# A third relu tile, 48 + 1 rows and a second store queue in a planned attention and long-convolution kernel

## The chip, the cores and the metric

The kernel runs on one core of one Trainium2 chip. The metric is the device time of one execution in microseconds (us). The median of three runs before the change is 1019.45 us (1018.49 to 1021.79).

## The reference

Eight batches of 3136 rows and 256 channels. Everything below is done for each batch.

```python
scores = (1 / S) * z @ z.T                     # z: 3136 x 64
out    = u * (np.maximum(scores, 0) ** 2 @ v)  # u, v: 3136 x 256
proj   = out @ w_proj                          # 256 -> 3 * 256
x1, x2, x3 = split(proj)
conv   = irfft(rfft(x2, axis=rows) * rfft(filter_fft, axis=rows))
y      = (x1 * conv * x3) @ w_out
```

## The kernel before

**Attention.** The 3136 rows of a batch are cut into seven chunks of columns (`CHUNKS`: five of 512, one of 256, one of 320), and the keys into 25 tiles of 128 rows, the last of 64. For a chunk, TensorE makes the scores of two key tiles at a time into a pair of PSUM banks (`ps_s`, three pairs). K is only 64 there, so the two tiles lie in the two halves of the array's rows: these matmuls use 64 rows of the array, and most others 128. ScalarE applies relu from PSUM into an f32 tile in SBUF, `R_p` (`relu`, L1759). The square goes from `R` to a bf16 tile `A_p` on VectorE (L1768) or on ScalarE (L1766), as the planner finds better; `relu` is for ScalarE alone. TensorE then weighs v with the squares into two accumulators, `ps_o` (one bank for each half of the 256 channels; `weigh`). Since scores are symmetric, a square of A is also turned by a DMA transpose on SP's queue (`mirror`, L1692) into `M1`, `M2e` or `M2o` and used by a later chunk. At the end of a chunk VectorE multiplies the accumulators with u, transposed by DMA, into `xT` (L1810); that frees the accumulators for the next chunk.

**Projection and convolution.** `add_proj` multiplies `xT` with `w_proj`: two of the three parts are multiplied into a gate tile (`g_p`, L1155), and the third goes through the first stage of a Fourier transform of length 49 x 64 (`dft1`) and is stored to a DRAM scratch, `spec`. When a batch's seven chunks are stored, `add_spectrum` loads that scratch in another order (`load_spec`, rows of one residue together: two times 49 partitions), does the second stage in eight groups of four quadrant matmuls ("quads", 49 or 64 rows, both banks of a pair), multiplies with the filter's transform on VectorE (L1240), does the inverse stage and stores (`put`). `add_end` loads the result by chunk (`load_c`), does the last stage, gates it (L1328), multiplies with `w_out` and stores to the output. PSUM is emptied by ScalarE (L551) or VectorE (L555), whichever the planner takes. The last batch has its own form: the eight groups are loaded one by one into whatever tiles are free, the inverse does the last addition on TensorE, and the chunks end in the order `FINAL`. Four chunks of the batch before it (`HOLD` and up) are held back and fill gaps there.

**The planner.** All of this is entered as tasks with a cost per engine, dependencies and tiles taken and freed (`Plan`). `Plan.go` then plays the engines forward and emits each instruction in the order that results; every engine gets a fixed list. `pick_pe` chooses TensorE's next task among queues: S (scores of a pair), Q (quads), W (weighing), FA, FB and FZ (projection, ends, fillers). It tries not to change between tasks of 64 rows (S, Q) and of 128 rows too often. `pick` chooses for the other engines. `Pairs` and `Singles` are the PSUM banks as the planner sees them; `MOST` is how many single banks may be held at once by tasks that take one. `PACE`, `BACKLOG`, `AMPLE`, `STAY`, `FULL`, `FIRST`, `LEAD` and `YIELD` are weights in these choices. SP's queue carries loads, stores and transposes in its planned order; POOL's carries the loads that convert from f32 to bf16 (v, u, z).

Of the kernel before, what the change touches and what calls it, by code (L numbers as in the profile page):

```python
# [11 lines left out]
P = 128  # L12
# [22 lines left out]
ZP, ZL = 0, 0.0  # L35
MOST = 4
FULL = 3.5
QUAD, FIRST, LEAD = -INF, 0.0, 1
YIELD = 1.0
REACH = 2  # L40
SHARE = {0: 1, 2: 3}

# [140 lines left out]
class Plan:  # L183
# [85 lines left out]
    def queued(self, t):  # L269
        some = {id(x): x for e in ("ACT", "DVE") for x in self.pend[e] if x.ready <= t + 0.3}  # L270
        return sum(max(0.0, self.free[e] - t) for e in ("ACT", "DVE")) + sum(min(x.cost.values()) for x in some.values())

    def pick_pe(self):
        t = self.free["PE"]
        got = {}
# [12 lines left out]
        if self.mode == "S" and self.quarters and quad and quad[0] <= t + STAY:  # L288
            if not more or self.quad_run < 1 and self.score_run >= LEAD:
                return (*quad, "Q")  # L290
        if more and not more[0].left:
            left = self.backlog()
            if self.mode == "S":
                if "S" in got and got["S"][0] <= t + STAY:
                    return (*got["S"], "S")
                got.pop("S", None)
                if self.quarters and quad and quad[0] <= t + STAY and self.quad_run < 1:
                    return (*quad, "Q")
            else:
                want = 3 if left > AMPLE else 2  # L300
                free = self.pairs.when(min(want, len(more)) - 1)
                first = quad and quad[0] <= t + 0.3 and left > FIRST and self.credit > QUAD
                if "S" in got and free > t + 0.04:
                    rest = {k: v for k, v in got.items() if k != "S" and (k == "W" or left > BACKLOG)}
                    if rest and min(v[0] for v in rest.values()) < free:
                        got = rest
                    elif free < INF:
                        if first and not LEAD:
                            return max(quad[0], free), quad[1], "Q"
                        self.soon = bool(first)  # L310
                        return max(got["S"][0], free), got["S"][1], "S"
                elif "S" in got:
                    if first and not LEAD:
# [10 lines left out]
        order += ["FA", "FB", "W", "FZ"] if self.credit > 0 and self.queued(t) < FULL else ["W", "FA", "FB", "FZ"]  # L324
# [28 lines left out]
    def go(self):  # L353
        while True:
# [11 lines left out]
            if k:  # L366
                self.queues[k].remove(task)
                half = k in ("S", "Q")
                if half != (self.mode == "S") and self.mode:
                    start += 0.095 if half or not self.quarters else 0.12  # L370
                    self.quarters, self.quad_run, self.score_run = half and self.soon, 0, 0
# [7 lines left out]
                if k == "W":  # L379
                    self.credit = min(self.credit + PACE, 2.0)  # L380
                elif k != "S":
# [7 lines left out]
def kernel(  # L389
# [587 lines left out]

    def by_row(d, r):
        return d[0:S, :].rearrange("(q r x) d -> r q x d", r=2, x=2 * NJ)[r]

    def load_spec(src, j0, nj, deps, late=0.0, home=l_p):
        box = {}

        def go():
            box["t"] = home.tile([P, 8, D] if home is l_p else [P, 4, D], BF16)
# [5 lines left out]
        t = on("SP", go, 0.9, [*deps, *((d, ISSUED) for d in loads[-1:])], [home.slots], moves=0.6 * nj, late=late)  # L991
        return in_order(t), box
# [216 lines left out]
    def add_spectrum(b, puts):  # L1209
        deps0 = list(h_done) + list(tz_done) if b == 0 else []  # L1210
        final = b == B - 1
        per = 2 if final else 4
        homes = [l_p, c_p, un_p] * 2 + M_p[:2]
        lasts = []
        behind = []
        ldb, gb = [None], [None]
        for g in range(NJ // 2):
            own = not final or g % 2 == 0
            xh, gh = (xh_p, (gs_p, uT_p)[final and g > 3]) if own else (R_p, A_p)
            if 2 * g % per == 0:  # L1220
                ldb[0] = load_spec(D1[b % 2], 2 * g, per, puts, LATE_LOAD * (not final), homes[g] if final else l_p)
            ld, ibox = ldb[0]
            ends_load = (2 * g + 2) % per == 0
            xb = {}

            def mm(ps, g=g, xb=xb, ibox=ibox, xh=xh):
                xb["x"] = xh.tile([P, 2, 4, D], BF16)
                forward(ps, slot(ibox["t"], 2 * g % per), g)

# [3 lines left out]
            a0, evs = add_quads(mm, ev, c_quads(g), [ld, *deps0], [xh.slots])  # L1233
            if ends_load:
                a0.frees.append((ld, 0))
# [15 lines left out]

            def inv(g=g, xb=xb, z_=z_, a0=a0, gh=gh):
                if 2 * g % per == 0:
                    gb[0] = {"es": [], "firsts": []}
                gx = gb[0]
                new = 2 * g % per == 0

# [9 lines left out]
                def ev(e, h, p, g=g):  # L1267
                    copy(e, gx["g"][:, ds(2 * (2 * g % per + h), 2), :].rearrange("p c d -> p (c d)"), p)

# [8 lines left out]
                gx["es"] += evs  # L1278
                if (2 * g + 2) % per:
                    return  # L1280
                j0 = 2 * g + 2 - per

                def put():
                    for r in range(2):
                        nc.sync.dma_start(
                            out=by_row(D2[b % 2], r)[:, ds(2 * j0, 2 * per), :], in_=gx["g"][ds(r * N1, N2), 0 : 2 * per, :]
                        )

                p_ = on("SP", put, 0.8, gx["es"], moves=0.5 * per, late=LATE_D2 * (not final))
                p_.frees.append((gx["g0"], 1))  # L1290
# [9 lines left out]
    def add_end(b, lasts, gtasks, cs, kind="FB", src=c_p, dsts=(o_p,), late=0, behind=(), then=(), split=False, mids=(y_p,)):  # L1300
        for at, c in enumerate(cs):
# [81 lines left out]

            def store(i0, n, c=c, ob=ob):
                r = rows_n1(out[b])
                for j, lo, hi, n2 in runs(T0[c] + i0, T0[c] + i0 + n):
                    nc.sync.dma_start(
                        out=r[:, n2 : n2 + hi - lo, :], in_=ob["o"][ds(j * N1, N1), i0 : i0 + hi - lo, :]
                    )
# [514 lines left out]
```

## Time and profile before

| | before |
|---|---|
| median of three runs | 1019.45 us |
| the profiled execution | 1014.12 us, span 1012.0 us |
| granted TensorE clock, mean | 0.988 |
| TensorE busy | 969.6 us (96%) |
| VectorE busy | 851.8 us (84%) |
| ScalarE busy | 854.2 us (84%) |
| relu from PSUM, 128 x 1024 (L1759) | 408 instructions, 1031 ns each |
| square on VectorE, 128 x 1024 (L1768) | 276 instructions, 1218 ns each |
| square on ScalarE, 128 x 1024 (L1766) | 116 instructions, 1072 ns each |
| DMA moved | 170.29 MB, mean 168 GB/s |

The time of the profiled execution includes about 2 us outside the span from the first to the last instruction. A duration in the table is one instruction from its start to its end; the next one on the same engine can start a little before that end. An engine's waits are put down to what released it.

### The profile page before, as it was taken

The numbers are of one execution on the slowest core, as the hardware profiler recorded it, in microseconds if no ns is written. First come the engines' busy times: TensorE is split into PE (matmuls) and PEld (weight loads), VectorE is DVE, ScalarE is ACT, GpSimd is POOL, SyncE is SP. The second block draws the span as 40 slices with busy tenths as digits, with TensorE's granted clock in tenths as the row PEclk, the third lists the DMA queues.
The fourth block names the chain that finished last, engine by engine and source line by source line (L and its number), as shares of the span: only waits on it lengthen the run. The fifth ranks groups of instructions, "written<-read, shape, count | busy, mean of one in ns | idle before, by whom it ended". The sixth has DMA issues, their size and how long they took to land.

```text
span 1012.0 us, 19360 instructions
## 1 busy us (share of the span) xinstructions
PE 969.6 (96%) x6776; PEld 472.2 (47%) x6776; DVE 851.8 (84%) x1470; ACT 854.2 (84%) x1182; POOL 187.5 (19%) x403
## 2 busy tenths in 40 slices
PE   6999999999999999999999999999999999999985
PEld 2343534446444653346544364434643455444744
DVE  7986699988899778988899688997789988998674
ACT  5886789897999789987889878997889978999673
POOL 5142311132011220313021131111301312000000
PEclk9999999999999999999999999999999999999978
DMA  9699788998999988987879999988899988977556
GB/s 168 130 165 166 121 156 165 165 137 187 185 194 174 196 163 168 172 170 140 203 171 138 170 163 188 196 152 172 186 176 173 162 148 195 173 166 130 158 182 207
DMA packets 331777, 170.29 MB, mean 168 GB/s; under 512 B 241160, under 2 KB 306504, under 8 KB 331680
## 3 DMA queue, kind: packets, MB, share of 16 engines
q1 hardware_dynamic: 303952, 138.09, 65.5%
q0 software_dynamic: 27728, 30.97, 21.6%
q8 instruction: 53, 0.87, 0.4%
q14 instruction: 44, 0.36, 0.1%
HBM read 90.26 MB, written 53.35 MB: 142 GB/s over the span
## 4 chain that ended last, share of the span: by engine, by line
PE 72%; DVE 11%; DMA 7%; ACT 5%; issue 3%; SPq 1%; ACTq 0%; DVEq 0%
PE ps_o_t L518 41%; PE ps_s L518 31%; DVE A_t L1768 5%; ACT R_t L1759 3%; DVE xT_t L1810 2%; DMA zT_t<-zd_t 2%; DMA M2e_t<-A_t 1%; ACT A_t L1766 1%; DVE xh L1240 1%; DMA spec_in_t<-spec 1%; DMA M_t<-A_t 1%; DMA conv_in_t<-spec 1%; DMA ost_t<-in_z_dram 1%; ACT gs_t L551 1%; DMA un_t<-spec 0%
## 5 line engine op out<-in xcount | busy, mean ns | idle before, releaser
L1759 ACT ACTIVATE R_t<-ps_s 128x1024 f32<-128x1024 f32 (+4 forms) x512 | 476.8, 960 | 79.9 <-PE ps_s L518 37.6
L518 PE MATMUL ps_o_t<-A_t,v_t 128*128 128x512 bf16 (+3 forms) x2068 | 463.5, 355 | 5.6 <-DVE A_t L1768 4.5
L1768 DVE TENSOR_TENSOR A_t<-R_t 128x1024 bf16<-128x1024 f32 (+3 forms) x337 | 379.9, 1145 | 56.0 <-ACT R_t L1759 45.7
L518 PEld LDWEIGHTS <-v_t 128*128 128x128 bf16 (+2 forms) x2872 | 247.6, 98 | 280.4 <-issue 87.4
L518 PE MATMUL ps_s<-zT_t 64*64 64x512 bf16 (+4 forms) x1436 | 174.5, 370 | 1.4 <-ACT R_t L1759 0.6
L1766 ACT ACTIVATE A_t<-R_t 128x1024 bf16<-128x1024 f32 (+4 forms) x159 | 153.0, 965 | 6.7 <-DMA M_t<-A_t 3.0
L601 POOL COPY tick<-xT_t 1x1 bf16<-1x1 bf16 x54 | 12.8, 237 | 720.1 <-DVE xT_t L1810 703.7
L551 ACT ACTIVATE x_t<-ps_s 128x512 bf16<-128x512 f32 (+2 forms) x169 | 91.8, 582 | 24.5 <-PE ps_s L518 19.1
L518 PEld LDWEIGHTS <-zT_t 64*64 64x64 bf16 (+1 forms) x1469 | 54.7, 100 | 119.6 <-issue 105.5
L518 PE MATMUL ps_s<-xT_t,wp 128*128 128x512 bf16 (+2 forms) x432 | 99.5, 353 | 2.4 <-DVE gate_t L1155 1.1
L1810 DVE SCALAR_TENSOR_TENSOR xT_t<-ps_o_t,uT_t 128x256 bf16<-128x256 f32 (+2 forms) x224 | 75.6, 380 | 13.5 <-PE ps_o_t L518 8.2
L1240 DVE TENSOR_TENSOR xh<-xh,H 128x1024 bf16<-128x1024 bf16 x120 | 81.7, 682 | 2.3 <-ACT xh L551 1.5
L518 PE MATMUL ps_o_t<-M_t,v_t 128*128 128x512 bf16 (+2 forms) x352 | 81.3, 353 | 0.0
L1155 DVE TENSOR_TENSOR gate_t<-ps_s,x_t 128x256 bf16<-128x256 f32 (+2 forms) x216 | 70.0, 380 | 9.9 <-PE ps_s L518 7.8
L1328 DVE TENSOR_TENSOR yT_t<-ps_s,gate_t 128x512 bf16<-128x512 f32 (+2 forms) x103 | 60.9, 619 | 10.7 <-PE ps_s L518 7.6
L518 PEld LDWEIGHTS <-wp 128*128 128x128 bf16 x448 | 43.6, 98 | 46.5 <-issue 8.8
L592 POOL DMA_DIRECT2D un_t<-in_u_dram x112 | 60.0, 556 | 7.5 <-issue 5.7
L611 POOL DMA_DIRECT2D v_t<-in_v_dram x112 | 59.5, 557 | 5.9 <-issue 3.2
L518 PE MATMUL ps_s<-wo,yT_t 128*128 128x256 bf16 (+1 forms) x364 | 53.4, 276 | 3.5 <-DVE yT_t L1328 2.0
L518 PE MATMUL ps_s<-wp,xT_t 128*128 128x256 bf16 x400 | 56.1, 273 | 0.3 <-DVE gs_t L555 0.2
L518 PE MATMUL ps_o_t<-M2e_t,v_t 128*128 128x512 bf16 (+1 forms) x192 | 46.9, 356 | 6.3 <-DVE xT_t L1810 6.2
L551 ACT ACTIVATE s_t<-ps_s 128x512 bf16<-128x512 f32 (+1 forms) x74 | 43.6, 599 | 6.4 <-issue 2.1
(145 smaller groups left out, 808.9 us busy)
## 6 DMA issues: line engine op xcount, KB each, us to landing
out_dram<-ost_t SPq DMA_DIRECT2D x66, 256.0 KB
spec<-s_t SPq DMA_DIRECT2D x96, 128.0 KB
spec_in_t<-spec SPq DMA_DIRECT2D x56, 196.0 KB
spec<-gs_t SPq DMA_DIRECT2D x56, 196.0 KB
v_t<-in_v_dram POOLq DMA_DIRECT2D x80, 128.0 KB, 5.0
un_t<-in_u_dram POOLq DMA_DIRECT2D x80, 128.0 KB, 5.2
conv_in_t<-spec SPq DMA_DIRECT2D x33, 256.0 KB
out_dram<-ost_t SPq DMA_DIRECT2D x19, 128.0 KB
```

The lines of the kernel that those rows point to most:

```text
L518: wrote(nc.tensor.matmul(o, *args, **kw), o)
L551: got = nc.scalar.activation(out_, in_, AF.Copy)
L592: nc.gpsimd.dma_start(out=t[ds(j * N1, N1), lo - t0 : hi - t0, :], in_=x[:, n2 : n2 + hi - lo, :])
L601: nc.gpsimd.tensor_copy(tick[:], xt["t"][0:1, 1, 0:1])
L611: nc.gpsimd.dma_start(out=t[ds(j * N1, N1), ds(v_at(a), (b - a) * D)], in_=r[:, n2 + a - lo : n2 + b - lo, :].rearrange("p t d -> p (t d)"),)
L1155: got = nc.vector.tensor_tensor(g[:, ::-1] if h == 0 else g, p, x, ALU.mult)
L1240: nc.vector.tensor_tensor(x[:, 1 - i], x[:, 0], h, ALU.mult)
L1328: got = nc.vector.tensor_tensor(yb["y"][:, dh, 0:w], p, gates[b, c, dh][:, 0:w], ALU.mult)
L1759: has_read(nc.scalar.activation(blocks(box["R"], n, cw)[:rows], p, AF.Relu), p)
L1766: nc.scalar.activation(a, r, AF.Square)
L1768: nc.vector.tensor_tensor(a, r, r, ALU.mult)
L1810: nc.vector.scalar_tensor_tensor(x, f, inv_s2, ut, ALU.mult, ALU.mult)
```

## The change

- The pool of relu tiles, `R_p`, has three tiles instead of two; the gate pool has 24 instead of 25; `MOST` is 3 instead of 4.
- The planner's weights become one rule, a named tuple that can differ by stretches of 50 us of planned time (here there is one rule for all): backlog 0.5 (was 1.0), ample 5 (was 99), stay 0.15 (was 0.05), pace 0.55 (was 0.5), give 0 (was 1.0, as `YIELD`). A change of row size is planned at 0.096 us in all cases.
- Loads and stores of the second stage move 48 rows for each half and the 49th row of both halves in a third transfer of two partitions.
- In the last batch the second stage loads two groups at a time into four tiles, and stores them as three pairs and two singles.
- The last batch's output stores, but for the last chunk's, go half to POOL's queue and half to SP's.

```diff
-BACKLOG, AMPLE, STAY = 1.0, 99.0, 0.05
-PACE = 0.5
-MOST = 4
-YIELD = 1.0
+MOST = 3
+Rule = namedtuple("Rule", "backlog ample stay first lead pace full give")
+STEP = 50.0
+RULES = [Rule(0.5, 5.0, 0.15, 0, 1, 0.55, 3.5, 0)]
...
-                want = 3 if left > AMPLE else 2
+                want = 3 if left > now.ample else 2
...
-                if end + YIELD * held >= max(self.free[first], task.ready) + behind + task.cost[first]:
+                if end + self.rule(t).give * held >= max(self.free[first], task.ready) + behind + task.cost[first]:
...
-    R_p = Pool("R", 2, [P, 2, 512], F32)
+    R_p = Pool("R", 3, [P, 2, 512], F32)
-    g_p = Pool("gate", 25, [P, 512], BF16)
+    g_p = Pool("gate", 24, [P, 512], BF16)
...
-    def by_row(d, r):
-        return d[0:S, :].rearrange("(q r x) d -> r q x d", r=2, x=2 * NJ)[r]
+    EVEN = N2 // NJ * NJ
+
+    def by_row(d, t, x0, n):
+        rows = d[0:S, :].rearrange("(q r x) d -> r q x d", r=2, x=2 * NJ)[:, :, ds(x0, n), :]
+        got = [(rows[r, 0:EVEN], t[ds(r * N1, EVEN), 0:n, :]) for r in range(2)]
+        return got + [(rows[:, EVEN], t[EVEN : EVEN + N1 + 1 : N1, 0:n, :])]
...
-            for r in range(2):
-                nc.sync.dma_start(
-                    out=box["t"][ds(r * N1, N2), 0 : 2 * nj, :], in_=by_row(src, r)[:, ds(2 * j0, 2 * nj), :]
-                )
+            for rows, part in by_row(src, box["t"], 2 * j0, 2 * nj):
+                nc.sync.dma_start(out=part, in_=rows)
...
-        per = 2 if final else 4
-        homes = [l_p, c_p, un_p] * 2 + M_p[:2]
+        sets = [(0, 1), (2, 3), (4, 5), (6,), (7,)] if final else [(0, 1), (2, 3), (4, 5), (6, 7)]
+        outs = [gs_p, gs_p, M_p[2], A_p, uT_p] if final else [gs_p] * 4
+        homes = [l_p, l_p, *M_p[:2]]
...
+            elif split:
+                s_ = on("POOL", lambda nt=nt, store=store: store(0, nt, (0,), nc.gpsimd), 0.6, [*oe, *behind], moves=0.22 * nt)
+                s_ = on("SP", lambda nt=nt, store=store: store(0, nt, (1,)), 0.8, [*oe, *behind], prio=1, moves=0.22 * nt)
```

More of the change, by code (lines that the diff above doesn't have):

```diff
@@ L1 @@
+from collections import namedtuple
 from contextlib import ExitStack
@@ L271, in queued, with rule @@
         return sum(max(0.0, self.free[e] - t) for e in ("ACT", "DVE")) + sum(min(x.cost.values()) for x in some.values())
+    def rule(self, t):
+        return RULES[min(int(t / STEP), len(RULES) - 1)]
     def pick_pe(self):
         t = self.free["PE"]
+        now = self.rule(t)
         got = {}
@@ L287, in pick_pe @@
         quad = got.pop("Q", None)
-        if self.mode == "S" and self.quarters and quad and quad[0] <= t + STAY:
-            if not more or self.quad_run < 1 and self.score_run >= LEAD:
+        if self.mode == "S" and self.quarters and quad and quad[0] <= t + now.stay:
+            if not more or self.quad_run < 1 and self.score_run >= now.lead:
                 return (*quad, "Q")
@@ L293, in pick_pe @@
             if self.mode == "S":
-                if "S" in got and got["S"][0] <= t + STAY:
+                if "S" in got and got["S"][0] <= t + now.stay:
                     return (*got["S"], "S")
                 got.pop("S", None)
-                if self.quarters and quad and quad[0] <= t + STAY and self.quad_run < 1:
+                if self.quarters and quad and quad[0] <= t + now.stay and self.quad_run < 1:
                     return (*quad, "Q")
             else:
-                want = 3 if left > AMPLE else 2
+                want = 3 if left > now.ample else 2
                 free = self.pairs.when(min(want, len(more)) - 1)
-                first = quad and quad[0] <= t + 0.3 and left > FIRST and self.credit > QUAD
+                first = quad and quad[0] <= t + 0.3 and left > now.first
                 if "S" in got and free > t + 0.04:
-                    rest = {k: v for k, v in got.items() if k != "S" and (k == "W" or left > BACKLOG)}
+                    rest = {k: v for k, v in got.items() if k != "S" and (k == "W" or left > now.backlog)}
                     if rest and min(v[0] for v in rest.values()) < free:
@@ L307, in pick_pe @@
                     elif free < INF:
-                        if first and not LEAD:
+                        if first and not now.lead:
                             return max(quad[0], free), quad[1], "Q"
@@ L312, in pick_pe @@
                 elif "S" in got:
-                    if first and not LEAD:
+                    if first and not now.lead:
                         return (*quad, "Q")
@@ L323, in pick_pe @@
         order = ["S", "Q"]
-        order += ["FA", "FB", "W", "FZ"] if self.credit > 0 and self.queued(t) < FULL else ["W", "FA", "FB", "FZ"]
+        order += ["FA", "FB", "W", "FZ"] if self.credit > 0 and self.queued(t) < now.full else ["W", "FA", "FB", "FZ"]
         for k in order:
@@ L369, in go @@
                 if half != (self.mode == "S") and self.mode:
-                    start += 0.095 if half or not self.quarters else 0.12
+                    start += 0.096
                     self.quarters, self.quad_run, self.score_run = half and self.soon, 0, 0
@@ L379, in go @@
                 if k == "W":
-                    self.credit = min(self.credit + PACE, 2.0)
+                    self.credit = min(self.credit + self.rule(start).pace, 2.0)
                 elif k != "S":
@@ L984, in go @@
         def go():
-            box["t"] = home.tile([P, 8, D] if home is l_p else [P, 4, D], BF16)
-            for r in range(2):
-                nc.sync.dma_start(
-                    out=box["t"][ds(r * N1, N2), 0 : 2 * nj, :], in_=by_row(src, r)[:, ds(2 * j0, 2 * nj), :]
-                )
-        t = on("SP", go, 0.9, [*deps, *((d, ISSUED) for d in loads[-1:])], [home.slots], moves=0.6 * nj, late=late)
+            box["t"] = home.tile([P, 8, D], BF16)
+            for rows, part in by_row(src, box["t"], 2 * j0, 2 * nj):
+                nc.sync.dma_start(out=part, in_=rows)
+        t = on("SP", go, 1.3, [*deps, *((d, ISSUED) for d in loads[-1:])], [home.slots], moves=0.6 * nj, late=late)
         return in_order(t), box
@@ L1218, in add_spectrum @@
             own = not final or g % 2 == 0
-            xh, gh = (xh_p, (gs_p, uT_p)[final and g > 3]) if own else (R_p, A_p)
-            if 2 * g % per == 0:
-                ldb[0] = load_spec(D1[b % 2], 2 * g, per, puts, LATE_LOAD * (not final), homes[g] if final else l_p)
+            xh = xh_p if own else R_p
+            mine = set_of[g]
+            per, gh = 2 * len(mine), outs[sets.index(mine)]
+            if g % 2 == 0:
+                ldb[0] = load_spec(D1[b % 2], 2 * g, 4, puts, LATE_LOAD * (not final), homes[g // 2] if final else l_p)
             ld, ibox = ldb[0]
-            ends_load = (2 * g + 2) % per == 0
             xb = {}
@@ L1227, in mm @@
                 xb["x"] = xh.tile([P, 2, 4, D], BF16)
-                forward(ps, slot(ibox["t"], 2 * g % per), g)
+                forward(ps, slot(ibox["t"], 2 * g % 4), g)
             def ev(e, h, p, xb=xb):
@@ L1250, in add_spectrum, with inv @@
             z_ = w_ if final else on("DVE", add, 2 * c_dve2(2 * D), [w_], prio=ZP)
-            def inv(g=g, xb=xb, z_=z_, a0=a0, gh=gh):
-                if 2 * g % per == 0:
+            def inv(g=g, xb=xb, z_=z_, a0=a0, gh=gh, mine=mine, per=per):
+                new = g == mine[0]
+                if new:
                     gb[0] = {"es": [], "firsts": []}
                 gx = gb[0]
-                new = 2 * g % per == 0
                 def mm(ps, g=g, new=new):
@@ L1278, in inv @@
                 gx["es"] += evs
-                if (2 * g + 2) % per:
+                if g != mine[-1]:
                     return
-                j0 = 2 * g + 2 - per
+                j0 = 2 * mine[0]
                 def put():
[L1284 to L1289, printed above, removed]
+                    for rows, part in by_row(D2[b % 2], gx["g"], 2 * j0, 2 * per):
+                        nc.sync.dma_start(out=rows, in_=part)
+                p_ = on("SP", put, 1.2, gx["es"], moves=0.5 * per, late=LATE_D2 * (not final))
                 p_.frees.append((gx["g0"], 1))
```

14 lines of the change are left out of this document (6 added, 8 removed).

## The prediction, made before the changed kernel was run

> **What bounds the kernel now.** I read the page's busy shares, then the stretches of the span, TensorE's waits, the groups, and last the end of the chain.
>
> ```profile
> span 1012.0 us, 19360 instructions
> PE 969.6 (96%) x6776; PEld 472.2 (47%) x6776; DVE 851.8 (84%) x1470; ACT 854.2 (84%) x1182; POOL 187.5 (19%) x403
> ...
> 60.00:545.00 485.00, 476.35 (x3285) 226.92 (x3282) 416.64 (x697) 418.67 (x575) 98.33 (x205) 1.00 0.89 169
> 545.00:595.00 50.00, 46.50 (x315) 22.36 (x314) 38.13 (x66) 39.51 (x57) 11.14 (x24) 0.97 1.01 149
> 595.00:955.00 360.00, 355.83 (x2539) 176.30 (x2538) 308.22 (x521) 320.10 (x439) 57.01 (x125) 1.00 0.89 172
> 955.00:1012.00 57.00, 41.41 (x383) 26.57 (x381) 35.48 (x74) 31.71 (x61) 0.00 (x0) 0.82 0.59 184
> ...
> 942.41 0.38 PE L518 MATMUL ps_o_t<-A_t,v_t 128*128 128x256 bf16 x2
> 942.73 0.45 PE L518 MATMUL ps_s<-zT_t 64*128 64x320 bf16 x4
> 943.11 0.61 PE L518 MATMUL ps_s<-wo,yT_t 128*128 128x256 bf16 x4
> ```
>
> The second group is stretches: length, then busy PE, PEld, DVE, ACT, POOL, the granted clock, the DMA share and GB/s. TensorE is busy 98% between 60 and 545 us and 99% between 595 and 955; it is the bound there, and the other two engines have about 14% of slack. Only the end, 57 us with TensorE busy for 41, is a chain.
>
> Busy is not all columns. Successive 512-column matmuls start 0.216 us apart. Counting every matmul's columns by its share of the array gives 867 us at that rate. The three timeline rows show the next cost: two 256-column matmuls (0.109 us each) should be over at 942.63, and the scores of 64 rows start at 942.73; four scores of 320 columns, two at a time, need 0.27 us, and the next full-array matmul comes 0.38 us after the first. Each change of row size costs 0.10 us or a little less (0.093 as the median of all). There are 545 of them, 51 us. Of the 1012 us, 867 + 51 = 918 is a floor of the instruction order; 94 is start, end and waiting. What waits from 60 to 955 us:
>
> ```profile
> PE ps_o_t L518 <- DVE xT_t L1810: 8.0, 9, 2.3
> PE ps_o_t L518 <- DVE A_t L1768: 2.8, 6, 0.6
> PE ps_s L518 <- ACT R_t L1759: 1.6, 3, 1.2
> PE ps_s L518 <- DVE xT_t L1810: 0.9, 3, 0.5
> PE ps_s L518 <- DVE yT_t L1328: 0.8, 1, 0.8
> ...
> ACT R_t L1759 <- DVE A_t L1768: 32.1, 51, 5.0
> ```
>
> TensorE waits for VectorE some 12.5 us here. ScalarE waits 32 us for a free R tile, but TensorE waits for ScalarE's R only 1.6 us: the third tile removes a long wait that is mostly not on the path.
>
> **Third R tile, MOST 3, the rule's new weights.** These act through the planner, so I compare instruction orders. The matmul columns are the same. Row-size changes fall from 545 to 514: 31 x 0.093 = 2.9 us less, with nothing beside it, since TensorE itself stands still. Against it stand 55 more, smaller matmuls (scores in 64-column pieces), about 14 groups of four; such a group takes 0.24 us where 0.216 would do, +0.3 us. Net -2.6 us.
>
> Squares move: 54 of 1024 elements go from VectorE to ScalarE, and 54 PSUM evictions of 512 elements go the other way. In unbroken runs of the trace a 1024 square starts 1.135 us (VectorE) or 0.947 us (ScalarE) before the next instruction, an eviction 0.60 or 0.477. VectorE: 54 x (1.135 - 0.60) = -29 us; ScalarE: 54 x (0.947 - 0.477) = +25 us, from 854 to about 879 (87%). Neither becomes the bound as a sum. What counts is the delay in front of TensorE. Of the 12.5 us that TensorE waits for VectorE, I take half as gone, -6 us: 52 fewer squares (of 346) stand ahead of the two evictions that free the accumulators. Bounds: -14 us, all of the waits in the list above, and +15 us if 16 of the 54 squares each hold up a relu that TensorE needs (16 x 0.947). I take a value on the gain's side because the one wait that ScalarE causes today is 1.6 us, against 12.5. At the start (first 60 us, VectorE busy 53) only one of the first 32 squares more goes to ScalarE: -1 us, between -3 and +2.
>
> **24 gate tiles.** In the instruction order at most 24 gates are live in both kernels, so one tile less changes nothing by itself; but the new order comes to 23 or 24 live gates in eleven of 25 stretches of VectorE's list, the old one in two. A projection then waits for an output's gating; that wait is 0.8 us in one place today. I put it at nothing, because the planner fills such a place with weighing matmuls; without that cover it is some 0.8 us per batch, 6 us in all, inside the range.
>
> **48 + 1 rows.** The trace's semaphore records show that a 49-row transfer (196 KB) lands in seven pieces, a 64- or 128-row one in sixteen. From issue to the last landing the 49-row load takes 5.5 us (median of 56), the 49-row store 5.0, a 128-row load of 256 KB 3.2. With 48 rows I expect about 3.2. It costs one more issue for each load or store, 49 more in all on SP's queue (some join others in the last batch), at 0.3 to 0.5 us: about 20 us of a queue that is idle more than a third of the time; behind it wait mirrors (1.2 to 1.7 us of issue each) and u's transposes. In the steady stretches TensorE waits 0.5 us in all for such loads, so a faster landing is hidden. It may avoid one accident: at 545.4 and 545.8 two 49-row stores are issued, take 6.7 and 8.2 us, and z's transpose behind them lands after 15.4 us; VectorE stands until 561.7, TensorE until 563.4 (its 2.3 to 2.5 us wait for xT), and the granted clock (0.97 in that stretch's row) is at half for 3.4 us just after. I count that accident within the 6 us.
> The Trainium skill ("TensorE: Matmul & The Clock Gate", "What's actually happening") lets the clock halve after an idle window of about 3.4 us; here a stall of 2.4 us was enough, so by the trace a short accident already costs more than its own length, by that rule it would not.
>
> **The last batch.**
>
> ```profile
> 960.51 1.63 DMA spec<-s_t
> 963.96 5.02 DMA un_t<-spec
> ...
> 982.36 0.59 ACT A_t L551
> 983.39 0.51 SPq L1285
> 984.33 0.55 SPq L1285
> 984.99 0.95 SPq L1285
> 985.99 3.93 DMA spec<-A_t
> 990.00 2.67 DMA A_t<-spec
> ...
> 1005.21 1.84 SPq L1387 DMA_DIRECT2D out_dram<-gs_t  x2
> 1007.15 1.82 SPq L1387 DMA_DIRECT2D out_dram<-xh  x2
> ```
>
> Loads: the third load (un_t) lands at 969.0. Four double loads of three issues replace eight of two; at 0.3 us an issue and 3.2 us to land, the same quarter is there 1.5 to 2 us sooner. But in the new order four output stores of 256 KB, 0.7 us of issue each, stand between the last first-stage store and these loads, 2.8 us where the landing waited for is 1.6. I take zero, between -2 and +2. Stores of the second stage: from the last eviction's end (982.95) to the landing (989.9) are 7.0 us; six issues at 0.4 and a landing of 2.4 (the 128 KB stores of sixteen pieces have 2.2) make about 5: -2 us, between -3 and 0. Last outputs: four SP issues of 0.92 us follow the last eviction; with three of them on SP and one on the POOL queue, -0.9 us, or 0 if POOL's store lands late (its loads take 5.0 us, which from 1005.2 would still be before the present end).
> The Trainium skill ("DMA: Bandwidth & Descriptors", "Issuing engines are not separate DMA queues") says that a second issuing engine saves sequencer time alone; 0.9 is all that this would leave here, and nothing for bandwidth. Sum of the end: -3 us.
>
> **Sum.** -2.6 - 6 - 1 - 3 = -12.6 us. The profiled execution took 1014.12 us (span 1012.0, 2.1 outside); the median shown, 1019.45, lies 5.3 above it. I carry the difference over: 1014.1 - 12.6 = 1001.5 for a profile, 1019.45 - 12.6 = 1007 us as the time.
>
> **Rivals.** (1) Off the path: ScalarE gets its tile sooner, TensorE's waits stay, the end's loads come as late as before, and only the 31 row-size changes and half the end are left: -2.6 - 1.5, about 1015. For it: 32 us of ScalarE's waits against 1.6 us of TensorE's. (2) A large gain: all 14 us of waits go, the end gives 6, the start 2, with 2.6: 995. For it: ScalarE never idles for a tile, score banks come free earlier. (3) Slower: relus queue behind squares on ScalarE. Each moved square ahead of a relu whose bank TensorE needs costs up to 0.947 us. From 13 such squares of 54 the gain of 12.6 is used up; from 17 on the kernel is measurably slower; at 24 it is +10, 1029.5. For it: ScalarE's share rises to 87% and relu runs on nothing else. Against it: 1.6 us of such waits now. (4) The parts cancel, with the gates' 6 us, a bad start, and the loads late: within the measurement, 1018.
>
> **Chances.** Forecast (1001 to 1012) 0.46; rival 1 0.17; rival 2 0.15; rival 3 0.15; rival 4 0.07. I call 0.3%, 3.1 us, the least that a measurement can tell from no change. Rivals 1 and 2 and the forecast are faster: 0.78. Same 0.07, slower 0.15. The range takes in the forecast, rivals 1 and 4, and the near halves of 2 and 3: 996 to 1022.
>
> **What would show it.** Right: TensorE's waits for xT_t and A_t halved, ScalarE's wait for R below 10 us, ScalarE at 86 to 88% of the span, no second spell of lower clock at mid-span, the stretch from 955 us shorter by 3. Wrong: PE ps_s <- ACT R_t among the first waits (rival 3); PE ps_s <- DVE yT_t at each batch's end (gates); SP issues of 48-row moves just before a late mirror, with A_t <- DMA waits above the present few us; or the loads of the last batch landing later than 8 us after the store before them.

## The result and the profile after

| | before | after |
|---|---|---|
| median, runs of one chip | 1018.97 us (1016.04 to 1021.79) | 993.21 us (992.0 to 993.85) |
| ratio, 95% interval | | 0.9746 [0.9716, 0.9776] |
| the profiled execution | 1014.12 us, span 1012.0 | 993.72 us, span 991.5 |

The kernel is faster by 25.8 us, about double the 12.6 forecast and below the range (996). The two profiled executions differ by 20.4 us; the other 5.4 is where each profile stands among its timed runs. The runs of before spread over 6 to 15 us in each group of runs, and its profile lies below the four timed ones of this table; the runs of after lie within 2 us.

The page of the kernel after, its stretches (columns as before: length, busy PE, PEld, DVE, ACT, POOL, granted clock, DMA share, GB/s), and TensorE's waits from 60 to 935 us. By equal work done on TensorE, 935 us here is 955 us of before.

```profile
span 991.5 us, 19534 instructions
PE 958.2 (97%) x6831; PEld 472.2 (48%) x6831; DVE 819.4 (83%) x1465; ACT 867.9 (88%) x1187; POOL 191.7 (19%) x409
...
545.00:595.00 50.00, 49.56 (x384) 25.66 (x382) 40.44 (x78) 48.02 (x70) 12.91 (x28) 1.00 0.79 151
...
60.00:935.00 875.00, 870.25 (x6174) 426.04 (x6172) 733.96 (x1284) 789.60 (x1068) 167.51 (x353) 1.00 0.88 171
935.00:991.50 56.50, 39.56 (x398) 25.86 (x395) 36.56 (x74) 31.50 (x60) 3.21 (x6) 0.83 0.72 209
...
PE ps_s L521 <- ACT R_t L1767: 0.9, 3, 0.4
PE ps_o_t L521 <- DVE A_t L1776: 0.8, 2, 0.4
PE ps_o_t L521 <- DVE xT_t L1818: 0.5, 1, 0.5
PE ps_s L521 <- DVE xT_t L1818: 0.4, 2, 0.2
```

TensorE is busy for 99.5% of the steady part. Its waits for VectorE (`xT`, `A` and `yT`), 12.5 us before, are 1.7. ScalarE's wait for a free R tile (32.1 us) is not among its waits any more. The stretch at 545 us, with a clock of 0.97 and 3.5 us of idle TensorE before, is now at 1.00 with 0.4 idle: the accident behind z's transpose is gone. The end is 56.5 us after 57.0.

Where the 20.4 us of the profiles went, by equal work: some 1 us up to 60 us, 19 in the steady part, 0.5 at the end. Of the 19, 2.9 are row-size changes (514 for 545, each 0.093). What TensorE spends in that part beyond its columns and these changes fell by some 16.6 us; 11.5 of these are single stalls of over 0.15 us.

### The profile page after: what moved, and what is told of

Read it like the earlier page. It is cut to its first block, busy times and chain, and to the rows that moved or that the text cites. A ratio compares the mean times of both kernels' runs of the same rounds, so it can differ in the third digit from the quotient of the medians.

```text
span 991.5 us, 19534 instructions
## 1 busy us (share of the span) xinstructions
PE 958.2 (97%) x6831; PEld 472.2 (48%) x6831; DVE 819.4 (83%) x1465; ACT 867.9 (88%) x1187; POOL 191.7 (19%) x409
## 4 chain that ended last, share of the span: by engine, by line
PE 82%; DVE 7%; ACT 4%; DMA 2%; issue 2%; SPq 1%; POOL 0%; POOLq 0%; DVEq 0%; ACTq 0%
PE ps_o_t L521 48%; PE ps_s L521 34%; DVE A_t L1776 2%; ACT R_t L1767 2%; DVE xT_t L1818 1%; DMA M2e_t<-A_t 1%; DVE xh L1248 1%; DMA ost_t<-in_z_dram 1%; DMA conv_in_t<-spec 1%; DVE gate_t L1160 1%; DVE yT_t L1334 1%; SPq L646 1%; ACT A_t L1774 0%; ACT x_t L554 0%; DMA M_t<-A_t 0%
## 5 line engine op out<-in xcount | busy, mean ns | idle before, releaser
L1767 ACT ACTIVATE R_t<-ps_s 128x1024 f32<-128x1024 f32 (+4 forms) x512 | 466.9, 963 | 57.1 <-PE ps_s L521 55.0
L521 PEld LDWEIGHTS <-v_t 128*128 128x128 bf16 (+2 forms) x2878 | 250.6, 98 | 257.8 <-issue 73.2
L1776 DVE TENSOR_TENSOR A_t<-R_t 128x1024 bf16<-128x1024 f32 (+3 forms) x283 | 313.9, 1123 | 64.2 <-ACT R_t L1767 61.1
L1774 ACT ACTIVATE A_t<-R_t 128x1024 bf16<-128x1024 f32 (+3 forms) x213 | 211.7, 1007 | 3.1 <-DMA M2e_t<-A_t 1.7
L521 PE MATMUL ps_s<-zT_t 64*64 64x512 bf16 (+5 forms) x1485 | 170.8, 361 | 2.0 <-ACT R_t L1767 1.0
L521 PE MATMUL ps_s<-xT_t,wp 128*128 128x512 bf16 (+2 forms) x430 | 103.7, 353 | 2.4 <-DVE gate_t L1160 0.9
L554 ACT ACTIVATE x_t<-ps_s 128x512 bf16<-128x512 f32 (+2 forms) x148 | 81.7, 583 | 19.7 <-PE ps_s L521 12.5
L1334 DVE TENSOR_TENSOR yT_t<-ps_s,gate_t 128x512 bf16<-128x512 f32 (+2 forms) x99 | 57.9, 613 | 10.3 <-PE ps_s L521 10.0
L558 DVE CAST xh<-ps_s 128x512 bf16<-128x512 f32 x71 | 47.3, 685 | 22.8 <-PE ps_s L521 19.5
```

The lines of the kernel that those rows point to most:

```text
L521: wrote(nc.tensor.matmul(o, *args, **kw), o)
L554: got = nc.scalar.activation(out_, in_, AF.Copy)
L558: got = nc.vector.tensor_copy(out_, in_)
L1334: got = nc.vector.tensor_tensor(yb["y"][:, dh, 0:w], p, gates[b, c, dh][:, 0:w], ALU.mult)
L1767: has_read(nc.scalar.activation(blocks(box["R"], n, cw)[:rows], p, AF.Relu), p)
L1774: nc.scalar.activation(a, r, AF.Square)
```

## The experiments

Two theories stood against each other. **A**: the third tile and the weights do it; the 48 + 1 rows are hidden, as the prediction had it. **B**: the 49-row transfers hold up the mirrors and other transposes queued behind them on SP, and the 48 + 1 rows free the steady part from that.

### Undoing one part of the change

49 rows in one transfer again, in the order of the kernel after on TensorE, VectorE and ScalarE:

```diff
-        got = [(rows[r, 0:EVEN], t[ds(r * N1, EVEN), 0:n, :]) for r in range(2)]
-        return got + [(rows[:, EVEN], t[EVEN : EVEN + N1 + 1 : N1, 0:n, :])]
+        return [(rows[r], t[ds(r * N1, N2), 0:n, :]) for r in range(2)]
```

> The changed kernel with the second stage's rows moved as 49 again (two transfers instead of 48, 48 and 2); the planner's costs and so the order of the computing engines are unchanged. Theory A (the planner's new order, from the third tile and the weights, took TensorE's waits away): within 3 us of the changed kernel, 993 to 997. Theory B (the 49-row transfers crowd seven DMA engines, delay transposes and so VectorE; their end is most of the gain of 26 us): 1005 to 1015, with runs that lie several us apart as those of the kernel before do.

Measured: 1011.43 us (1005.56 to 1014.3), ratio 0.9928 [0.9899, 0.9957]. So 18 of the 25.8 us are lost without this edit, and A, which expected 993 to 997, falls. Its profile is of one of its quickest runs (1006.4) and shows 12.7 of the 18. The SP queue in this kernel, then its chain of waits (start, duration, what), then VectorE's waits for transposes from 60 to 935 us and a wait of TensorE:

```profile
92.19 1.68 SPq L993 DMA_DIRECT2D spec_in_t<-specf  x4
93.98 1.24 SPq L1699 DMA_TRANSPOSE M2e_t<-A_t  x1
...
96.80 6.81 SPq L1699 DMA_TRANSPOSE M2e_t<-A_t  x1
...
93.98 8.03 DMA M2e_t<-A_t
...
102.10 0.97 DVE A_t L1775
...
110.98 10.16 DMA M_t<-A_t
...
663.68 7.71 DMA zn_t<-in_z_dram
...
DVE A_t L1775 <- DMA M2e_t<-A_t: 5.5, 1, 5.5
...
DVE A_t L1775 <- DMA M_t<-A_t: 3.5, 1, 3.5
...
PE ps_s L521 <- DVE H L560: 2.9, 1, 2.9
```

The same place of the queue in the kernel after, and its one such wait:

```profile
91.62 3.02 SPq L994 DMA_DIRECT2D spec_in_t<-specf  x6
94.75 1.24 SPq L1700 DMA_TRANSPOSE M2e_t<-A_t  x1
...
99.17 2.19 SPq L1700 DMA_TRANSPOSE M2e_t<-A_t  x1
...
DVE A_t L1776 <- DMA M_t<-A_t: 1.1, 1, 1.1
```

Read from top to bottom: four 49-row loads are issued, the mirror right behind them lands 8.0 us after its issue (5.9 in the kernel after, from the landing records), and the next mirror's issue is stuck for 6.8 us (2.2 there). The A tile of that mirror can't be written again before it has landed, so VectorE's square waits 5.5 us, and ScalarE's next relu 4.5 us for the R tile that the square holds. What stands behind the square in VectorE's order is late too, and TensorE waits 1.6 us for an `xT`. Behind the next four loads the mirror lands after 10.2 us (8.5 in the kernel after, where late mirrors are fewer but not gone), VectorE waits 3.5 us, and TensorE 2.9 for a bank that VectorE empties (`H`).

By equal work, TensorE loses 6.0 us between 101 and 153 us and 3.6 between 635 and 682. In each of the two the granted clock is at 0.50 for 3.4 us (from 123.5 and from 673.0 us), right behind stalls of 2.9 and 1.7 us.

The second loss doesn't come from SP's queue. It hangs on a load of z on POOL's queue (`zn_t` above) that lands after 7.7 us; the same load took 5.3 in the kernel after. All runs show the same two marks. With 49 rows (before, e1, e7, e9, e10), 29 to 49 of the 260 transposes take over 6 us to land, and v's loads of 128 KB on POOL's queue 4.9 to 5.6 us by the median. In the ten kernels with 48 + 1 rows these are 9 to 20 transposes and 4.0 to 4.6 us. So B is too narrow: transfers that don't stand behind the 49-row ones on SP are late too.

Two R tiles, and the planner counts two:

```diff
-    R_p = Pool("R", 3, [P, 2, 512], F32)
+    R_p = Pool("R", 2, [P, 2, 512], F32)
```

> The changed kernel with two R tiles, planned anew. Theory A with the third tile as its main part: 1005 to 1012, ScalarE waiting some 30 us for VectorE's squares again and TensorE some 8 us for xT. Theory A with the weights as its main part: 995 to 1000. Theory B: 994 to 998.

Measured: 1006.48 us (1004.0 to 1009.02), 0.989 [0.9868, 0.9913]: the tile is worth 13 us in the new kernel. That is outside B's range (994 to 998) and inside one of A's (1005 to 1012), so neither theory holds alone. The waits that A expected did not come: ScalarE waits 2.4 us for VectorE's squares, not 30, and TensorE 0.5 for `xT`, not 8. TensorE's first wait from 60 to 935 us:

```profile
PE ps_o_t L521 <- DVE A_t L1776: 3.9, 10, 0.8
```

Without the tile TensorE waits for squares (3.9 us in this row, and 2.1 for ScalarE's squares in the next; 0.8 in all with it). That is 5 of the 13 us; the rest is spread over the span and not placed. Row-size changes stay at 513: fewer changes are the work of the weights, not of the tile.

The old weights and `MOST` 4 in the new kernel:

```diff
-MOST = 3
+MOST = 4
...
-RULES = [Rule(0.5, 5.0, 0.15, 0, 1, 0.55, 3.5, 0)]
+RULES = [Rule(1.0, 99.0, 0.05, 0, 1, 0.5, 3.5, 1.0)]
```

> The changed kernel with the old weights and MOST 4, planned anew; three R tiles stay. Row-size changes should be near 545 again, +2.9 us. Theory A with the weights as main part: 1003 to 1010. Theory A with the tile as main part: 995 to 1000. Theory B: 994 to 999.

Measured: 999.02 us (996.35 to 1002.33), 0.9826 [0.98, 0.9852], 5.8 slower than the kernel after, at the upper edge of what B and the form of A with the tile as its main part expected; 555 row-size changes against 514 (3.8 us by 0.093 each).

### One part alone, in the kernel before

The 48 + 1 rows as in the change, first everywhere, then (e5) everywhere but in the last batch's own form, whose groups are loaded one by one (`if n < 8: return` the two 49-row transfers):

> The kernel before with rows as 48, 48 and 2; costs and order of the computing engines as before. Theory A: 1015 to 1020, no gain that can be told from its spread. Theory B: 1000 to 1010, the runs closer together, and no stop of VectorE behind a transpose of over 10 us.

> The kernel before with rows as 48, 48 and 2 in every batch but the last, which keeps its 49-row transfers; costs and computing order as before. In the run with 48 rows everywhere the work before the last batch's end was 5.8 us shorter and the end 6.1 us longer. Theory B (48 rows are worth several us in any order, and three issues for each single group cost the end): 1008 to 1012, and less spread than the kernel before. Theory A (only the new order needs them): 1015 to 1018.

Measured: 1016.09 us (1013.89 to 1018.78), 0.9976 [0.9952, 0.9999], and 1012.17 us (1008.12 to 1013.98), 0.9941 [0.9915, 0.9967]. The first lies where A expected it and not B (1000 to 1010), the second just above B's 1012. In the profile of the first, the work up to the last batch ends 5.8 us sooner and the end is 6.3 longer. In that of e5 the end is 2.3 longer; the other 4 fit three issues for each of eight single groups in SP's way there, which no run shows by itself. Where groups go in pairs, the edit alone brings 5.7 us.

In the profiles nearly all of that comes at one place: between 540 and 600 us, where e4 gains 5.6 of its 5.8 us. It is the accident that the prediction named. Two rows of before, then the stretch of it and a wait in e4:

```profile
DVE A_t L1768 <- DMA M_t<-A_t: 5.5, 2, 5.3
...
DVE zd_t L1460 <- DMA zT_t<-zd_t: 3.5, 2, 3.3
```

```profile
545.00:595.00 50.00, 49.82 (x369) 26.09 (x369) 42.81 (x80) 43.83 (x65) 12.90 (x28) 1.00 0.86 159
...
DVE A_t L1768 <- DMA M_t<-A_t: 4.3, 1, 4.3
```

TensorE was busy for 46.50 us of this stretch before, at a clock of 0.97. The transpose of z, behind two 49-row stores, lands after 15.4 us before and 11.4 in e7 (49 rows, same order); behind the 48 + 1 rows it takes 6.0 in e4 and 4.5 in e5. VectorE's longest wait for a mirror, on the other hand, loses only 0.9 us (5.3 us until 85.7 us before, 4.3 in e4), and TensorE's wait for `xT` right behind it as much (2.3 to 1.4).

The third tile alone, three times. In e7 it is there but the planner counts two (and 25 gates, of which 24 exist), so the order is that of before; in e10 the planner counts it; e9 has the weights and `MOST` alone.

```diff
-    R_p = Pool("R", 2, [P, 2, 512], F32)
+    R_p = Pool("R", 3, [P, 2, 512], F32)
+    R_p.slots = Slots(2)      # e7 only
...
-    g_p = Pool("gate", 25, [P, 512], BF16)
+    g_p = Pool("gate", 24, [P, 512], BF16)
+    g_p.slots = Slots(25)     # e7 only
```

> The kernel before in its own order, with a third R tile and 24 gates in memory while the planner still counts two and 25. Theory A (the tile works through the order that the planner makes with it): 1013 to 1018, ScalarE's 32 us of waits for VectorE's squares nearly gone, TensorE's waits as they were. If the tile itself is what helps: 1003 to 1010.

> The kernel before with the four new weights of the planner (0.55, backlog 0.5, ample 5, stay 0.15), three as the limit in place of four and the new price of a row-size change; two R tiles, 25 gate tiles, 48 and 49 rows in one transfer, old last batch. If the weights bring their 6 us by themselves (they brought 5.8 in the new kernel): 1012, ratio 0.994, with the waits of TensorE for VectorE's xT_t and A_t near the 12.5 us of before and fewer row-size changes (about 514). If they only pay once the third tile stands behind them: 1016 to 1020, ratio 0.998 to 1.002. If they pay only without the 49-row transfers, the same 1016 to 1020, with an accident of 4 to 6 us behind a slow transpose in the steady part.

> The kernel before with the third tile and 24 gate tiles, which the planner counts, and nothing else. The tile alone, in the old order, brought 5.4 us. If that is all that it does: 1012.5, ratio 0.995. If the planner's own use of it brings the rest of the 13 us that it was worth in the new kernel: 1005, ratio 0.987, with VectorE's waits on R gone and TensorE's waits for xT_t and A_t under 4 us. If the 49-row transfers eat it, as they ate 18 us of the new kernel: 1013 to 1018 with one or two stalls of 3 to 6 us behind a DMA in the steady part.

Measured: e7 1012.49 us (1006.59 to 1016.22), 0.9935 [0.9906, 0.9965]; e9 1015.42 us, 0.9984 [0.9958, 1.0011]; e10 1011.44 us (1007.29 to 1012.72), 0.9934 [0.9908, 0.9961]. So in the old kernel the tile brings some 6 us whether it is planned or not (e7 lies between its two expected ranges), and the weights nothing that can be told from no change. Three readings of waits from 60 to 935 us. First e9, with two tiles, ScalarE's wait for VectorE's squares and the longest of TensorE:

```profile
ACT R_t L1759 <- DVE A_t L1768: 1.0, 2, 0.5
...
PE ps_o_t L518 <- DVE A_t L1768: 5.3, 8, 1.7
```

The weights alone take ScalarE's 32 us of waits for a tile down to 1.0, by giving it more of the squares (it is busy 897 us, 854 before), and the time does not move; but TensorE's other waits are new ones in this order. Then e7, in the order of before:

```profile
ACT R_t L1761 <- DVE A_t L1770: 2.8, 1, 2.8
```

Here the third tile takes 29 of the 32 us away, and the time falls by 5.4. So that wait was mostly not on the path, as the prediction said. Of the 6.2 us between the profiles of before and e7, 2.8 come at the accident of 546 us, so the tile's gain and the rows' gain are in part the same one. Then e10, with three tiles and 49 rows:

```profile
DVE A_t L1768 <- DMA M2e_t<-A_t: 7.8, 4, 3.1
...
PE ps_s L518 <- DMA conv_in_t<-spec: 4.5, 3, 2.1
...
DVE A_t L1768 <- DMA M_t<-A_t: 3.0, 1, 3.0
```

TensorE's waits for VectorE are down to some 3 us (12.5 before), and what stands out instead lands late: loads that TensorE waits for (4.5 us, 0.3 before) and mirrors that VectorE waits for (10.8 us, 9.3 before). 38 of 260 transposes take over 6 us.

### Together, without the last batch

The e5 kernel with tile, gates, weights and `MOST` 3:

> The kernel before with the third R tile, 24 gates, the new weights, MOST 3 and 48-row transfers in all but the last batch: all of the change but its last batch (paired loads, sets of stores, POOL's queue), and with the old costs of SP's transfers in the plan. If the last batch's new form is worth nothing, as the two stretches at the end say (57.0 and 56.5 us): 991 to 996. If it is worth the 3 us forecast: 996 to 999.

Measured: 995.79 us (993.95 to 1000.41), 0.9782 [0.974, 0.9824]. Tile and weights bring 16.4 us on top of the 48 rows, where alone they bring 6 and nothing. The new form of the last batch is the rest, 2.6 us, which the two intervals don't tell from nothing. Why tile and weights bring so much more with the 48 rows no run shows by itself; a tighter order with less slack for late transfers would fit.

### Rows or issues

e1 also has fewer issues on SP. To part the two, four transfers for each group in three cuts, with the same issues and the same orders on TensorE, VectorE and ScalarE; `EVEN` is 48, 44 and 35:

```diff
-        got = [(rows[r, 0:EVEN], t[ds(r * N1, EVEN), 0:n, :]) for r in range(2)]
-        return got + [(rows[:, EVEN], t[EVEN : EVEN + N1 + 1 : N1, 0:n, :])]
+        cuts = ((0, EVEN), (EVEN, N2 - EVEN))
+        return [(rows[r, q : q + m], t[ds(r * N1 + q, m), 0:n, :]) for q, m in cuts for r in range(2)]
```

> Control for the next two: the kernel after with 48 rows and the 49th row of each half moved apart, so four transfers for each group in place of three (48, 48, 1, 1). The orders of TensorE, VectorE and ScalarE are those of the kernel after. If the number of rows that an engine has to move decides, this is the kernel after but for one more issue on SP for each group, in which SP is not late in the steady part: 993 to 996, ratio 0.975 to 0.978. If SP's issues decide, some 50 more of them cost 10 us or more: above 1003.

> The same four transfers and the same orders, cut as 44 rows and 5 rows. By the theory that a transfer is spread over as many engines as divide its rows (at most 16; 49 rows lay on seven), 44 lie on eleven with four rows each, and 5 on five: between the control and 49 rows, 995 to 1000, and the transposes that land later than 6 us (18 of 260 in the kernel after, 49 with 49 rows) 20 to 35. If the 48-row cut brings its gain only by the number of transfers or by SP's timing: the same as the control.

> The same four transfers and the same orders, cut as 35 rows and 14 rows. By the same theory 35 lie on seven engines with five rows each, and 14 on fourteen: close to 49 rows on seven engines with seven rows each (1011.4), 1000 to 1010, with stalls of TensorE behind transposes near 95 to 125 us, where the transfers of 49 rows cost two transposes of 8 and 10 us. If the number of transfers or SP's timing brings the gain: the same as the control.

| cut | pieces of the larger part, rows in each | time, us | ratio, 95% interval | transposes over 6 us |
|---|---|---|---|---|
| 48 + 1 (e13) | 16, three | 993.1 (992.41 to 994.52) | 0.977 [0.9745, 0.9795] | 12 |
| 44 + 5 (e14) | 11, four | 992.69 (992.49 to 995.44) | 0.9774 [0.9747, 0.98] | 16 |
| 35 + 14 (e15) | 7, five | 1000.38 (998.45 to 1002.64) | 0.9847 [0.9818, 0.9876] | 20 |
| 49 (e1) | 7, seven | 1011.43 (1005.56 to 1014.3) | 0.9928 [0.9899, 0.9957] | 49 |

The pieces are the landing records of a transfer: sixteen for 48 rows; 12 for 44 rows and eight for 35 and 49, of which the first comes 0.5 us after the issue, well before the others (1.9 us or later), and is taken for no landing. The number of issues costs nothing (e13 is as fast as the kernel after). The time goes with the rows in a piece: three or four are free, which e14 did not expect, five cost 7 us and seven 18. The places expected for e15 were wrong as well: it loses nothing before 670 us and all of it from there on, with a u transpose of 7.24 us on its chain at 699 us.
The Trainium skill ("DMA: Bandwidth & Descriptors", "Why a DMA increments its semaphore by 16 and not by 1") has a transfer spread over the largest number of engines, up to 16, that divides the slowest dimension of both its sides: 16 for 48 rows, 11 for 44, 7 for 35 and for 49. The trace agrees, with as many pieces.

### The last batch

All the last batch's outputs on SP again (the POOL branch left out), and POOL's queue for the first four chunks only:

```diff
-            elif split:
+            elif split and c in cs[:4]:      # e11; the branch is absent in e8
```

> The changed kernel with the last batch's outputs all on SP's queue. In the changed kernel all data has landed at 987.9 us, and the span ends at 991.5 because POOL's last drain runs 8.4 us from its last store. If that drain costs what it seems to (2.7 us after SP is done) and the second queue saves 0.9 us: 991 to 992, span end 1.1 us after the last landing. If the second queue is worth the 0.9 us forecast: 994.

> The kernel after with the last batch's outputs on POOL's queue for its first four chunks only; the stores of the two chunks behind them go back to SP. The orders of TensorE, VectorE and ScalarE are the same as in the kernel after. If POOL's drain behind its last store (8.4 us, ending 2.9 us after all data had landed) is what the second queue costs: the drain starts some 6 us sooner and no longer ends the span; 991.2, ratio 0.973 to 0.975, span end 1.1 us behind the last landing. If the second queue costs by something else (POOL's stores hold up the loads or outputs): unchanged, 993.

Measured: 991.73 us (990.83 to 995.12), 0.9743 [0.9699, 0.9787], and 990.62 us (989.6 to 991.53), 0.9739 [0.9713, 0.9766], against 993.21 for the kernel after. The ratios (0.9746 after) don't tell the three apart; e11's runs (989.6 to 991.53) all lie below those of the kernel after, e8's overlap them. The spans of the profiles are 991.5, 989.0 and 989.2 us, so the second queue costs some 2.4 us there, where its last store is late. POOL's last store and the last link of the chain in the kernel after, then the last link in e11:

```profile
982.33 0.53 POOL L1394 DMA_DIRECT2D out_dram<-gs_t  x1 [0.61 <-ACT gs_t L554]
...
982.31 0.55 POOLq L1907
```

```profile
982.10 0.49 ACTq L1907
```

In the kernel after, the chain ends on POOL: behind its last store its closing drain takes 8.4 us (982.31 to 990.76 in the records), while the last data landed at 987.85 us and SP was done at 988.1. With POOL's last store 3.4 us sooner (at 978.89), the span ends 0.9 us behind the last landing (988.28), not 3.7. The trace of before has this drain as well: 7.7 us behind POOL's last load, from 936.6 us, where it ended long before the span did.

The last batch's loads ahead of two of the four output stores that stand before them on SP, with all outputs on SP:

```diff
...
+                        for s_ in held_s[1:]:
+                            join(s_, last_spec[0], ISSUED)
...
```

> The kernel after with all the last batch's outputs on SP's queue (991.7 measured) and two output stores of the batch before it put behind the last batch's loads on SP, where they had stood ahead of them. If these loads wait for SP's issues (each 0.7 to 0.9 us): they are issued 1.3 to 2 us sooner, the last batch's stage starts that much sooner, and the time is 989.5 to 990.5, ratio 0.972, the best of all the runs. If the loads wait for the landing of the last first-stage put instead, or if the last batch has other work to cover: 991.7.

Measured: 991.88 us (990.75 to 994.57), 0.9756 [0.9728, 0.9784]: nothing gained against e8, where 989.5 to 990.5 was expected if the loads wait for SP. The first load is issued at 937.4 us instead of 940.7. The chain some 20 us later:

```profile
958.61 0.58 ACT M2o_t L554
959.19 0.35 ACT ost_t L554
959.56 0.51 SPq L1396
...
960.11 1.30 SPq L1396
...
961.51 0.52 SPq L1293
```

The tile of the second store of the stage (`M2o_t`) is full at 959.2 us, but its issues start at 961.5: two output stores came between. What was taken from ahead of the loads is given back ahead of a store of the same stage. The lowest medians are those of e8, e11 and e12, 990.6 to 991.9 us, which can't be told from each other.

## Why the prediction was right or wrong

**What bounds the kernel.** Right. TensorE's own waits were the thing to count, and ScalarE's 32 us were mostly off the path: e7 took 29 of them away in the old order and gained 5.4.

**Row-size changes, -2.6 us.** Right in size: 514, as the order said, worth 2.9. They come from the weights (e3 555, e2 513).

**VectorE waits half gone, -6 us.** A term that was mis-sized. 12.5 became 1.7, so -10.8, close to its bound of -14, and shorter waits fell as well. Some 4 of the 10.8 come with the rows alone (8.5 are left in e4). With the changes and the start the forecast had 9.6 us for tile and weights; on top of the 48 rows they measured 16.4. What the prediction set against the gain, relus behind squares on ScalarE, cost 0.9 us (TensorE's wait for R), less than before; rival 3 had no start.

**48 + 1 rows, nothing by themselves.** The step that failed. The prediction priced these transfers by TensorE's direct waits for loads (0.5 us), and the accident at 546 us by TensorE's wait in it (2.3 to 2.5 us), inside another term. The rows are worth 5.7 us in the old order (e5) and 18 in the new one (e1). In the old order the profiles have nearly all of it at that one accident, at more than twice the price: 5.6 us. TensorE stalled for 2.2 us and then had half the granted clock for 3.4 us, which by estimate is another 1.7; the rest is not placed. In the new order, 49 rows make mirrors, z's transposes and POOL's loads late at other places as well, and VectorE passes the delay on. VectorE's own waits for mirrors, 9.3 us before, show this path (TensorE's 2.3 us for `xT` at 87.7 us stand behind one of 5.3), but not the price: 6.0 of them are left with the 48 + 1 rows (e4).

**The parts add up.** They don't. Rows alone 5.7, tile alone 6.4, weights alone nothing that can be told, 12 in all; together 22.1 (e6). Tile and weights with 49 rows and the new last batch (e1) are no faster than the tile alone (e10), 1011.4 both.

**The median's offset, 5.3 us, carried over.** Wrong: the profile after lies within 0.5 us of its median. Part of the scatter goes with the 49-row transfers (e1's runs spread over 8.7 us, e13's over 2.1), not all of it (e3's over 6.0, with 48 + 1 rows).

**The end, -3 us.** -0.5 in the profiles. The second stage's stores did better than their -2: from the last eviction's end to the landing are 3.7 us (963.22 to 966.96) for 7.0 before. Their working had a misreading without effect: 2.2 us is the median of the 64 KB stores, the 96 `spec` stores of 128 KB have 3.6. For the loads, nothing speaks against the zero (e12: where they are issued sooner, the time stays). The POOL queue's -0.9 had the wrong sign, some +2.4 in the profiles, by POOL's drain. The prediction left it out; the trace of before has it (7.7 us), hidden. The Trainium skill ("DMA: Bandwidth & Descriptors", "Issuing engines are not separate DMA queues"), which the prediction named, has a second issuing engine save the time of issuing alone. The trace agrees: the last data land at 987.85 us with it and at 987.82 without (e8).

**24 gates, nothing.** The list of TensorE's waits in the steady part after has neither a gate nor `yT` as a releaser, so that cover held.

Rival 2, the large gain, came nearest (995). It was right on TensorE's waits in the steady part, but it had nothing for the rows and 6 us for an end that gave 0.5, so that its number came near is partly luck.

Open: no run shows the pieces of one transfer on their engines. That the longer pieces of 49 rows hold up other transfers, on SP's queue and POOL's, is what the four cuts and the landing times fit best, not something seen. The count of slow transposes follows the cuts, but not in step with the time (20 for 7 us, 49 for 18). Each kernel has one trace, and the runs of those with 49 rows spread by several us, so how often an accident like that at 546 us happens stays open.

## What to carry to other kernels

Price a transfer by what is in flight with it and behind it, not only by who waits for it: follow each tile that a late DMA writes or reads until the engine that is full loses time, and count the slow clock after the stall too. Move rows in counts that spread over many pieces; 49 = 48 + 1 cost one issue more and was worth 18 us in the new order. When several edits each remove a small wait of a full engine, add nothing up until the waits that they uncover have been looked for. A second queue for the last stores can cost time unless its own drain ends before the other queue's last landing; look for that drain in the trace before the change.

## What the runs showed of the hardware

- POOL's closing drain took 8.4 us behind its last store, and the span then ended 3.7 us after the last landing; with outputs on SP alone it ended 1.2 us after (e8). The drain took 7.7 us in the kernel before and 8.7 in e11.
- A transfer of 48 rows of 4 KB landed in 4.1 us (load) and 3.1 us (store) by the median, one of 49 rows in 5.5 and 5.0 before; 44 rows in 4.3 and 3.2, 35 rows in 4.6 and 3.4.
- Four 49-row loads issued in 1.7 us: the next two mirrors landed 8.0 us after their issue, and the issue of the second took 6.8 us on SP's queue where 1.2 is usual (5.9, 4.0 and 2.2 us with 48 + 1 rows).
- With 49 rows on SP's queue, loads of 128 KB on POOL's queue landed in 4.9 to 5.6 us by the median of each kernel, with 48 + 1 rows in 4.0 to 4.6.
- Stalls of TensorE of 2.2 us (before) and of 2.9 and 1.7 us (e1) were each followed by 3.4 us at half the granted clock; one of 2.3 us, at 87.7 us before, was not.
